# A token table made on chip by one-hot products in place of scattered writes, with gathers paced by relus

## The chip, the cores and the metric

The kernel runs on one NeuronCore of one Trainium2 chip. The metric is device time in microseconds (us). The kernel before has a median of 384.94 us in 3 runs (384.61 to 385.42). Its profile is one more execution, taken by the hardware profiler; that one took 421.93 us, of which 420.1 us lie between the first and the last instruction.

The engines are named as the profile names them: PE is TensorE's matmuls and PEld its weight loads, DVE is VectorE, ACT is ScalarE, POOL is GpSimd, and SP is SyncE, which here only issues transfers.

## What is computed

Two stages follow each other: attention with a relative position bias, and then a mixture of eight experts in which a hash of each token's id names its expert. Shapes: batch 8, 8 heads, 576 positions, head dimension 64; 4608 tokens of width 512; 8 experts with a hidden width of 1024.

```python
# attention, cut
scores = scale * np.matmul(q, k.transpose(0, 1, 3, 2))
scores = scores + bias.transpose(2, 0, 1)[None, :, :, :]
scores = scores - np.max(scores, axis=-1, keepdims=True)
attn = np.exp(scores)
attn = attn / (np.sum(attn, axis=-1, keepdims=True) + 1e-09)
attn_out = np.matmul(attn, v)
# (B, H, S, D) becomes x of (B * S, H * D); then the experts:
expert_idx = token_ids * np.int64(2654435761) % np.int64(E)
for e in range(E):
    mask = expert_idx == e
    xe = x[mask]
    h = np.maximum(xe @ w1[e], 0.0)
    out[mask] = h @ w2[e]
```

Because the multiplier is odd and E is 8, the low three bits of a token's id settle its expert.

## The kernel before

The attention stage walks through 32 pairs of heads (8 batches of 4 pairs; pair n). For each pair it goes through five groups g: TensorE makes the scores, ScalarE takes the exponential, VectorE multiplies the part near the diagonal by the exponential of the bias ("band"), and TensorE multiplies the result of the pair before by v ("av"), which VectorE divides by the row sum and writes to x_all. VectorE also converts q and k to fp16 and empties the transposes from PSUM.

A routing generator `route()` is advanced by one step after the scores of a group, in pairs 2 to 7 at most. It gives every token a slot: 640 slots for each expert (CAP), 5120 in all (NSLOT). ds2 holds the slot of each token, 128 partitions by 40 columns.

```python
def route():
    ...                       # expert of each token, its rank within the expert
    nc.vector.scalar_tensor_tensor(
        out=ds2[:, :], in0=ovf[:, :], scalar=float(BIG),
        in1=sel[:, :], op0=ALU.mult, op1=ALU.add,
    )
    yield
```

From the slots the kernel needs the opposite: for each slot, which row of x belongs there and which row of the output it goes to (the two differ, since positions are stored in a permuted order). It writes this table to memory with 40 scatters of 128 entries of 8 bytes, and reads it back as xid:

```python
def name_slot(g):
    i = nc.gpsimd.indirect_dma_start(
        out=id_d.ap()[:, :],
        out_offset=bass.IndirectOffsetOnAxis(ap=ds2[:, g : g + 1], axis=0),
        in_=pay[:, g, :], in_offset=None,
        bounds_check=NSLOT - 1, oob_is_err=False,
    )
...
for n in range(NP + 1):
    ...
    if b + 1 < B and m == 3:
        cast_vs(b + 1)              # on GpSimd
    if n >= 8:
        for g in unnamed[:3]:
            name_slot(g)
        del unnamed[:3]
    if n == 27:
        nc.sync.dma_start(out=xid[:, :, :],
                          in_=id_d.ap().rearrange("(g p) c -> p g c", p=P))
    ...
    for g in range(NIT):            # NIT is 5
        scores(n, g)
        if 2 <= n < 8:
            next(routing, None)
        if g == 0:
            transpose_k(n + 1)      # PSUM tile pk, tag "aux"
            band(n - 1, NIT - 1)
            advance(av, 13)
        elif g == 1:
            cast_v(n + 2)
            cast_k(n + 2)
            advance(av, 14)
            band(n, 0)
        elif g == 2:
            cast_q(n + 3)
            advance(av, 9)
            band(n, 1)
        elif g == 3:
            transpose_q(n + 2)      # PSUM tile pq, tag "aux"
            band(n, 2)
            advance(av, 99)
        else:
            band(n, 3)
```

The tag "aux" has two PSUM buffers, which pk, pq and the two tiles px of each pair's av take in turn:

```python
def aux(shape, dtype, name):
    return atp.tile(shape, dtype, name=name, tag="aux", bufs=2,
                    space=bass.MemoryType.PSUM)
```

In the expert stage, GpSimd gathers the rows of x for each expert (five gathers of 128 rows), TensorE transposes them, the hidden layer runs in eight groups ft that each end in a relu on ScalarE, and the second layer's results are scattered to the output:

```python
xn = {0: x_load(0)}
xt = {0: x_transpose(xn[0])}
xn[1] = x_load(1)
for e in range(E):
    if e + 2 < E:
        xn[e + 2] = x_load(e + 2)
    for ft in range(NFT):                 # 8
        ...                               # 8 matmuls into hps
        nc.scalar.activation(..., func=AF.Relu, ...)
    if e + 2 < E:
        load_w1(e + 2)
    if e + 1 < E:
        xt[e + 1] = x_transpose(xn[e + 1])
    for kc in range(NSC):                 # 5
        ...                               # 8 matmuls into ops, a copy to ok
        so = nc.gpsimd.indirect_dma_start(out=out[:, :], ...)
    if e + 2 < E:
        load_w2(e + 2)
```

Of the kernel before, what the change touches and what calls it, by code (L numbers as in the profile page):

```python
# [11 lines left out]
F32 = mybir.dt.float32  # L12
F16 = mybir.dt.float16
# [18 lines left out]
def kernel(  # L32
# [11 lines left out]
    nc = tc.nc  # L44
# [37 lines left out]
    I128_np[:PB, P:] = np.eye(PB)[:, ::-1]  # L82
    CNT_np = np.ones((P, 2 * P), dtype=np.float16)
    CNT_np[:, :P] = np.tril(CNT_np[:, :P])
    UA, UB = 2 * HALF // 3, HALF // 3
    tok_of = np.concatenate([
# [6 lines left out]
    for t in range(NIT):  # L93
# [11 lines left out]
        np.tile(np.arange(E, dtype=np.float32), (P, 1)),  # L105
    ], axis=1)

# [7 lines left out]
    x_d = nc.dram_tensor("t5_x", [N, DM], F16, kind="Internal")  # L115
    id_d = nc.dram_tensor("t5_id", [NSLOT, 2], I32, kind="Internal")

# [12 lines left out]
    flag = cst.tile([1, 1], I32, name="flag")  # L130
    cst.tile([P, 48], I32, name="gap1")

    def disjoint(x, group):
        i = getattr(x, "ins", x)
        tc.declare_no_dep(
            i, group=group,
            reason="each token has a row of its own, so these writes are disjoint",
        )
        tc.add_to_no_dep_group(group, i)
# [23 lines left out]
    with tc.tile_pool(name="at", bufs=1) as at, tc.tile_pool(  # L163
# [25 lines left out]
        tef = at.tile([P, S], F16, name="tef")  # L189
        cnt = at.tile([P, 2 * P], F16, name="cnt")  # L190
        msk = at.tile([P, NGT + E], F32, name="msk")

# [60 lines left out]
        def route():  # L253
# [14 lines left out]
            for t in range(NIT):  # L268
# [17 lines left out]
                in0=ef[:, :].unsqueeze(1).to_broadcast([P, E, NGT]),  # L286
                in1=msk[:, NGT:].unsqueeze(2).to_broadcast([P, E, NGT]),
                op=ALU.is_equal,
# [5 lines left out]
                           space=bass.MemoryType.PSUM)  # L294
            nc.tensor.matmul(out=rps[:, 0, :EN], lhsT=cnt[:, P:], rhs=ohf)
            nc.tensor.matmul(out=rps[:, 1, :EN], lhsT=cnt[:, :P], rhs=ohf)
# [43 lines left out]
                out=ds2[:, :], in0=ovf[:, :], scalar=float(BIG),  # L340
                in1=sel[:, :], op0=ALU.mult, op1=ALU.add,
            )
            yield
# [153 lines left out]

        def name_slot(g):
            i = nc.gpsimd.indirect_dma_start(  # L499
                out=id_d.ap()[:, :],  # L500
                out_offset=bass.IndirectOffsetOnAxis(
                    ap=ds2[:, g : g + 1], axis=0
                ),
                in_=pay[:, g, :],
                in_offset=None,
                bounds_check=NSLOT - 1,
                oob_is_err=False,
            )
            disjoint(i, "ids")

        def store(b, t0, t1):
# [106 lines left out]
        for i in range(1, 4):  # L618
            v_init(i)
        nobody = at.tile([P, NSLOT // P, 2], I32, name="nobody")  # L620
        nc.gpsimd.memset(nobody[:, :, :], BIG)
        load_bias(nc.gpsimd, 0, 1, 0)
        load_bias(nc.sync, 0, 1, 1)
        for b2 in range(2):
# [20 lines left out]
        )  # L645
        nc.gpsimd.dma_start(
            out=id_d.ap().rearrange("(p g) c -> p (g c)", p=P),
            in_=nobody[:, :, :].rearrange("p g c -> p (g c)"),
        )
        for i in range(3):  # L650
            nc.gpsimd.memset(xg[i][:, :, :].bitcast(I32), 0)

        NP = len(pairs)
        unnamed = list(range(NGT))
        routing = route()
# [4 lines left out]
        for n in range(NP + 1):  # L660
# [15 lines left out]
            if n >= 8 and pairs[n][1] == 0:  # L676
                store(pairs[n - 8][0], 0, NIT)
            if n >= 8:
                for g in unnamed[:3]:
                    name_slot(g)  # L680
                del unnamed[:3]
            if n == 27:
                nc.sync.dma_start(
                    out=xid[:, :, :],
                    in_=id_d.ap().rearrange("(g p) c -> p g c", p=P),
                )
            if n == 20:
# [7 lines left out]
            for g in range(NIT):  # L695
                scores(n, g)
                if 2 <= n < 8:
                    next(routing, None)
# [42 lines left out]
            if n == NP - 1:  # L741
                band(n, NIT - 1)
        assert not unnamed and next(routing, None) is None
        guard.__exit__(None, None, None)

    with tc.tile_pool(name="mo", bufs=1) as mo, tc.tile_pool(
# [5 lines left out]

        def x_load(e):
            xpn = xg[e % 3]
            for sc in range(NSC):
                nc.gpsimd.indirect_dma_start(  # L756
                    out=xpn[:, sc, :],
                    out_offset=None,
                    in_=x_d.ap()[:, :],
                    in_offset=bass.IndirectOffsetOnAxis(  # L760
                        ap=xid[:, NSC * e + sc, 0:1], axis=0
                    ),
                    bounds_check=N - 1,
                    oob_is_err=False,
                )
            return xpn
# [21 lines left out]
        xt = {0: x_transpose(xn[0])}  # L788
        xn[1] = x_load(1)
        for e in range(E):  # L790
            if e + 2 < E:
                xn[e + 2] = x_load(e + 2)
            w1h, w2h = w1t[e % 2], w2t[e % 2]
            h1 = mo.tile([P, NFT, CAP], F16, name="h1", bufs=2)
            for ft in range(NFT):
                hps = mop.tile([P, NRC, 512], F32, name="hps", bufs=2,
                               space=bass.MemoryType.PSUM)
                for nr in range(NRC):
# [9 lines left out]
                    in_=hps[:, :, :NR], func=AF.Relu, bias=0.0, scale=1.0,  # L808
                )
            if e + 2 < E:  # L810
                load_w1(e + 2)
            if e + 1 < E:
                xt[e + 1] = x_transpose(xn[e + 1])
            for kc in range(NSC):
# [20 lines left out]
                )  # L835
                disjoint(so, "orows")
            if e + 2 < E:
                load_w2(e + 2)
# [129 lines left out]
```

## Time and profile before

| What | Value |
|---|---|
| time, median of 3 | 384.94 us |
| span in the profile | 420.1 us |
| attention, up to the last store of x | about 237 us of the span |
| first matmul of the expert stage's hidden layer | 249.1 us |
| scatters of the table (40, GpSimd) | 45.7 us busy, 1.14 us each, between 51.8 and 157.3 us |
| gathers of x (40, GpSimd) | 40.8 us busy, 1.02 us each |
| scatters of results (40, GpSimd) | 39.5 us busy, 0.99 us each |

How to read it: the page gives each engine's busy time, then the span in 40 slices of 10.5 us with a digit for the busy share of each. The groups list the instructions by line, their shape, how often they ran, busy time and mean duration, and then how long the engine had been idle before them and what ended that wait. A timeline row has the start in us from the span's beginning, the duration in us, the engine and the instruction; in brackets stands the idle time before it and what it waited for. "Issue" there is time in which the engine waited for nothing that the profile shows.

### The profile page before, as it was taken

How to read it: one execution, taken by the hardware profiler on the slowest of the kernel's cores; microseconds unless marked ns; L12 is line 12 of the kernel's file. 1: busy time of each engine (PE TensorE's matmuls, PEld its weight loads, DVE VectorE, ACT ScalarE, POOL GpSimd, SP SyncE). 2: the span in 40 equal slices, each digit the busy share in tenths (PEclk: the TensorE clock that was granted, in tenths of full speed). 3: DMA queues.
4: the chain of work that ended last, by engine and by line, in shares of the span. 5: the costliest groups of instructions: out<-in, count | busy, mean ns of one | idle time of the engine just before them, and what ended most of it. 6: DMA issues, size and time to landing. Idle time of an engine off the chain costs nothing.

```text
span 420.1 us, 8668 instructions
## 1 busy us (share of the span) xinstructions
PE 340.8 (81%) x3433; PEld 241.1 (57%) x3433; DVE 232.7 (55%) x646; ACT 220.4 (52%) x258; POOL 167.5 (40%) x193
## 2 busy tenths in 40 slices
PE   2778887966865878889988456999999999999992
PEld 1457665755754767777777334564646465656550
DVE  4688885965963989999997320313141413132211
ACT  1676766965954879999999202241405050414230
POOL 5570171372372180010100175265747474640422
PEclk9898896995995999999999958999999999999997
DMA  8999646564553659899990132669798999997212
GB/s 196 235 240 250 154 104 155 141 131 119 148 113 112 155 128 183 205 238 246 198 190 3 59 95 75 107 163 206 183 209 179 218 196 205 184 203 107 111 43 84
DMA packets 124436, 65.88 MB, mean 157 GB/s; under 512 B 85215, under 2 KB 116600, under 8 KB 124386
## 3 DMA queue, kind: packets, MB, share of 16 engines
q0 software_dynamic: 19456, 31.94, 36.2%
q1 hardware_dynamic: 104834, 33.18, 33.2%
q8 instruction: 29, 0.48, 0.5%
q14 instruction: 21, 0.17, 0.2%
q10 hardware_dynamic: 96, 0.11, 0.1%
HBM read 68.26 MB, written 15.30 MB: 199 GB/s over the span
## 4 chain that ended last, share of the span: by engine, by line
PE 40%; issue 20%; ACT 14%; POOL 8%; DMA 7%; DVE 6%; SPq 2%; POOLq 1%; another core or an unknown queue 0%; ACTq 0%
ACT att L402 11%; PE hps L800 9%; PE ops L818 9%; PE px L473 8%; PE ps L394 7%; POOL out_dram L826 4%; DMA kf<-in_k_dram 4%; PE ps L398 3%; POOL xg L756 3%; ACT vt L246 3%; DMA xg<-t_x,xid 2%; PE pk L367 2%; PE xps L774 1%; DVE att L435 1%; DVE x_all L484 1%
## 5 line engine op out<-in xcount | busy, mean ns | idle before, releaser
L402 ACT ACTIVATE att<-ps 128x1152 f16<-128x1152 f32 x128 | 141.4, 1129 | 52.9 <-PE ps L398 40.8
L806 ACT ACTIVATE h<-hps 128x640 f16<-128x640 f32 x64 | 45.1, 704 | 124.9 <-PE hps L800 100.6
L394 PE MATMUL ps<-qt,kz 128*128 128x384 f16 x256 | 79.3, 348 | 28.4 <-ACT att L402 21.2
L473 PE MATMUL px<-vt,att 128*128 128x98 f16 x1280 | 86.8, 213 | 4.8 <-DVE x_all L484 2.4
L473 PEld LDWEIGHTS <-att 128*128 128x128 f16 x1280 | 74.1, 102 | 11.5 <-issue 4.0
L800 PE MATMUL hps<-xpt,w1t 128*128 128x320 f16 x512 | 75.1, 309 | 3.3 <-issue 2.3
L435 DVE TENSOR_TENSOR att<-att,ebd 128x384 f16<-128x384 f16 (+2 forms) x224 | 71.1, 354 | 3.7 <-ACT att L402 3.6
L818 PE MATMUL ops<-w2t,h 128*128 128x512 f16 x320 | 70.4, 379 | 0.0
L800 PEld LDWEIGHTS <-w1t 128*128 128x128 f16 x512 | 51.5, 101 | 26.7 <-issue 4.1
L398 PE MATMUL ps<-qt,kz 128*128 128x192 f16 x256 | 66.4, 260 | 0.0
L826 POOL DMA_INDIRECT out_dram<-ok,xid x40 | 39.5, 987 | 63.9 <-DVE ok L825 63.6
L756 POOL DMA_INDIRECT xg<-t_x,xid x40 | 40.8, 1020 | 50.3 <-DMA t_x<-x_all 38.4
L778 DVE COPY xpt<-xps 128x512 f16<-128x512 f16 x40 | 15.7, 421 | 80.5 <-PE xps L774 78.4
L825 DVE COPY ok<-ops 128x512 f32<-128x512 f32 x40 | 27.7, 691 | 52.0 <-PE ops L818 52.0
L818 PEld LDWEIGHTS <-h 128*128 128x128 f16 x320 | 31.0, 98 | 36.0
L499 POOL DMA_INDIRECT t_id<-pay,ds x40 | 45.7, 1141 | 12.1 <-issue 11.0
L224 POOL CAST vs<-vsf 64x256 f16<-64x256 f32 x16 | 8.8, 550 | 104.3 <-PE px L473 62.4
L398 PEld LDWEIGHTS <-kz 128*128 128x128 f16 x256 | 26.2, 102 | 33.8 <-issue 33.7
L473 PE MATMUL px<-vs,atts 128*128 128x132 f16 x160 | 36.3, 227 | 1.5 <-issue 1.2
L394 PEld LDWEIGHTS <-kz 128*128 128x128 f16 x256 | 26.2, 102 | 13.2 <-issue 2.9
L484 DVE TENSOR_TENSOR x_all<-px,rcp 128x256 f16<-128x256 f32 x64 | 31.4, 491 | 2.2
L774 PE MATMUL xps<-ident,xg 128*128 128x128 f16 x160 | 15.0, 229 | 15.8 <-DMA xg<-t_x,xid 12.1
(67 smaller groups left out, 289.7 us busy)
## 6 DMA issues: line engine op xcount, KB each, us to landing
qf<-in_q_dram SPq DMA_DIRECT2D x32, 288.0 KB
kf<-in_k_dram SPq DMA_DIRECT2D x32, 288.0 KB
vf<-in_v_dram SPq DMA_DIRECT2D x64, 128.0 KB
w1t<-in_moe_w_dram POOLq DMA_DIRECT2D x8, 1024.0 KB
w2t<-in_moe_w_dram POOLq DMA_DIRECT2D x8, 1024.0 KB
t_x<-x_all SPq DMA_DIRECT2D x7, 512.0 KB
vsf<-in_v_dram SPq DMA_DIRECT2D x16, 64.0 KB
t_id<-pay,ds POOLq DMA_INDIRECT x40
```

Of the source, the lines that this page charges most:

```text
L394: nc.tensor.matmul(out=ps[:, hh, :QW], lhsT=kt, rhs=qt[:, :QW], start=True, stop=True,)
L398: nc.tensor.matmul(out=ps[:, 2, RW * hh : RW * hh + RW], lhsT=kt, rhs=qt[:, QW:], start=True, stop=True,)
L402: nc.scalar.activation(out=att[:, g, :, :], in_=ps[:, :, :QW], func=AF.Exp, bias=0.0, scale=scale,)
L435: nc.vector.tensor_tensor(out=a, in0=a, in1=ebd[:, :, m, :, a0 + w0 : a1 + w0].transpose([0, 2, 1, 3]), op=ALU.mult,)
L473: nc.tensor.matmul(out=px[:, ii, o : o + w], lhsT=lhsT, rhs=rhs, start=(y == 0), stop=(y == len(todo) - 1), skip_group_check=True,)
L484: nc.vector.tensor_tensor(out=x_all[:, b, its[0] : its[0] + ni, P * m : P * m + P].rearrange("p t (h d) -> p t h d", h=2), in0=pv[:, :, :, ...
L499: i = nc.gpsimd.indirect_dma_start(out=id_d.ap()[:, :], out_offset=bass.IndirectOffsetOnAxis(ap=ds2[:, g : g + 1], axis=0), in_=pay[:, g, ...
L756: nc.gpsimd.indirect_dma_start(out=xpn[:, sc, :], out_offset=None, in_=x_d.ap()[:, :], in_offset=bass.IndirectOffsetOnAxis(ap=xid[:, NSC * ...
L800: nc.tensor.matmul(out=hps[:, nr, :NR], lhsT=w1h[:, kt, ts(ft, P)], rhs=xt[e][:, kt, ts(nr, NR)], start=(kt == 0), stop=(kt == NPT - 1),)
L806: nc.scalar.activation(out=h1[:, ft, :].rearrange("p (r n) -> p r n", r=NRC), in_=hps[:, :, :NR], func=AF.Relu, bias=0.0, scale=1.0,)
L818: nc.tensor.matmul(out=ops[:, :], lhsT=h1[:, ft, ts(kc, P)], rhs=w2h[:, ft, :], start=(ft == 0), stop=(ft == NFT - 1),)
L826: so = nc.gpsimd.indirect_dma_start(out=out[:, :], out_offset=bass.IndirectOffsetOnAxis(ap=xid[:, NSC * e + kc, 1:2], axis=0), in_=ok[:, : ...
```

## The change

The table is no longer written to memory and read back. Two one-hot factors are made on VectorE for each batch: ph says which partition a token's slot lies in, and rh which of the 40 columns. TensorE multiplies them, so that the product holds, at each slot, the token's position plus one and its batch; VectorE adds up the eight batches and turns the sums into the two columns of xid. The step of xid's second column (the output row) follows the permutation by thresholds. The steps are appended to `route()`, which now goes on at two steps for each pair (after the scores of groups 1 and 3) from pair 5.

In the expert stage, the gathers for a later expert are issued one by one, each after a tiny copy on GpSimd that reads a value of the relu's output and so waits for that relu. The gathers for expert 2 come after expert 0's results. The purpose is to take the scatters out of the attention loop and to avoid long runs of gathers.

```diff
@@ in route(), behind ds2 @@
+            part = at.tile([P, 2, NGT], I32, name="part")
+            col = at.tile([P, 2, NGT], F16, name="col")
+            nc.vector.tensor_scalar(out=part[:, 0, :], in0=ds2[:, :],
+                scalar1=P - 1, scalar2=None, op0=ALU.bitwise_and)
+            nc.vector.tensor_scalar(out=part[:, 1, :], in0=ds2[:, :],
+                scalar1=P.bit_length() - 1, scalar2=None, op0=ALU.arith_shift_right)
+            yield
+            nc.vector.tensor_scalar(out=col[:, :, :], in0=part[:, :, :],
+                scalar1=1000.0, scalar2=None, op0=ALU.min)
+            acc = at.tile([P, 2, NSG], F32, name="acc")
+            yield
+            for b in range(B):
+                ph = at.tile([P, NIT, P], F16, name="ph", tag="ohsb")
+                rh = at.tile([P, NIT, 2, NSG], F16, name="rh", tag="ebsb")
+                cb = ...                          # col of this batch
+                nc.vector.tensor_tensor(out=ph[:, :, :],          # 640 elements
+                    in0=cnt[:, 2 * P : 3 * P].unsqueeze(1).to_broadcast([P, NIT, P]),
+                    in1=cb[:, 0, :].unsqueeze(2).to_broadcast([P, NIT, P]),
+                    op=ALU.is_equal)
+                yield
+                nc.vector.tensor_tensor(out=rh[:, :, 1, :],       # 200 elements
+                    in0=cnt[:, 3 * P :].unsqueeze(1).to_broadcast([P, NIT, NSG]),
+                    in1=cb[:, 1, :].unsqueeze(2).to_broadcast([P, NIT, NSG]),
+                    op=ALU.is_equal)
+                yield
+                nc.vector.tensor_tensor(out=rh[:, :, 0, :], in0=rh[:, :, 1, :],
+                    in1=msk[:, NGT + E :].unsqueeze(2).to_broadcast([P, NIT, NSG]),
+                    op=ALU.mult)
+                nc.vector.tensor_scalar(out=rh[:, :, 1, :], in0=rh[:, :, 1, :],
+                    scalar1=float(b), scalar2=None, op0=ALU.mult)
+                yield
+                nps = aux([P, 2, NSG], F32, "nps")
+                for t in range(NIT):
+                    nc.tensor.matmul(out=nps[...], lhsT=ph[:, t, :], rhs=rh[:, t, :, :],
+                                     start=(t == 0), stop=(t == NIT - 1))
+                if b == 0:
+                    nc.vector.tensor_copy(out=acc[:, :, :], in_=nps[:, :, :])
+                else:
+                    nc.vector.tensor_tensor(out=acc[:, :, :], in0=acc[:, :, :],
+                        in1=nps[:, :, :], op=ALU.add)
+                yield
+            ...                    # ep (2 operations), xid's column 0, tk
+            for i in steps:        # three places where the permutation jumps
+                ...                # tm, and tk = tk + tm
+                yield
+            ...                    # xid's column 1 from tk
@@ in the loop over pairs @@
-            if n >= 8:
-                for g in unnamed[:3]:
-                    name_slot(g)
-                del unnamed[:3]
-            if n == 27:
-                nc.sync.dma_start(out=xid[:, :, :], in_=id_d...)
-                if 2 <= n < 8:
+                if n >= 2 and (n < 5 or g in (1, 3)):
                     next(routing, None)
@@ in the expert stage @@
-        xn[1] = x_load(1)
         for e in range(E):
-            if e + 2 < E:
-                xn[e + 2] = x_load(e + 2)
             for ft in range(NFT):
                 ...                               # matmuls and relu
+                later = e + 2 if e > 0 else 1
+                if later < E and ft < NSC:
+                    nc.gpsimd.tensor_copy(out=pace[:, :], in_=h1[:1, ft, 0:1])
+                    xn[later] = x_load(later, ft)     # one gather
             ...
+            if e == 0:
+                xn[2] = x_load(2)
```

Also removed are the table in memory, its fill and the tile for that; the constants cnt and msk grow by the numbers that the one-hots are compared and weighted with.

## The prediction

> **What bounds the kernel now.** I read the page first, then busy time by window, the groups with shapes kept apart, and the timelines of ScalarE, TensorE and VectorE.
>
> ```profile
> span 420.1 us, 8668 instructions
> PE 340.8 (81%) x3433; PEld 241.1 (57%) x3433; DVE 232.7 (55%) x646; ACT 220.4 (52%) x258; POOL 167.5 (40%) x193
> ...
> DVE  4688885965963989999997320313141413132211
> ...
> PEclk9898896995995999999999958999999999999997
> ```
>
> The averages mislead: VectorE is busy 55% of the span, but its row of slices reads 9 wherever the attention loop is undisturbed. By windows of 20 us:
>
> ```profile
> core 0: us, PE busy (x) PEld busy (x) DVE busy (x) ACT busy (x) POOL busy (x), PEclk, DMA share, GB/s
> 120.00:140.00 20.00, 11.51 (x126) 8.99 (x123) 9.66 (x30) 9.48 (x11) 7.08 (x8) 0.74 0.44 111
> 180.00:200.00 20.00, 17.26 (x257) 14.21 (x254) 19.41 (x62) 18.69 (x22) 0.00 (x0) 1.00 1.03 237
> ```
>
> The second window is the loop at its steady rate: VectorE 19.41 of 20 us. ScalarE's last exponential of each head pair gives that rate:
>
> ```profile
> 176.56 0.66 ACT L414 ACTIVATE atts<-ps 128x576 f16<-128x576 f32 x1
> 182.36 0.66 ACT L414 ACTIVATE atts<-ps 128x576 f16<-128x576 f32 x1
> 188.15 0.66 ACT L414 ACTIVATE atts<-ps 128x576 f16<-128x576 f32 x1
> ```
>
> One pair is 5.79 us. Who sets it? VectorE's timeline (start, duration):
>
> ```profile
> 184.65 0.55 DVE L240 CAST kh<-kf 96x768 f16<-96x768 f32 x1
> 185.23 0.18 DVE L483 RECIPROCAL rcp<-px 128x4 f32<-128x4 f32 x1
> 185.45 0.42 DVE L484 TENSOR_TENSOR x_all<-px,rcp 128x256 f16<-128x256 f32 x1
> 185.79 0.48 DVE L435 TENSOR_TENSOR att<-att,ebd 128x128 f16<-128x128 f16 x2
> 186.19 0.55 DVE L231 CAST qh<-qf 96x768 f16<-96x768 f32 x1
> 186.66 0.62 DVE L435 TENSOR_TENSOR att<-att,ebd 128x384 f16<-128x384 f16 x2
> ```
>
> No idle time stands on any of these lines: each instruction starts before the one ahead has reported its end, or 0.03 us after. So VectorE sets the pair, with no slack I can find. ScalarE waits some 0.5 us a pair. TensorE streams about 11,000 columns a pair (scores 5184, products with v 4580, transposes 1248); at 0.136 us per 320 columns (expert stage: 64 matmuls in 8.69 us by the chain) that is 4.6 us.
>
> The first window is different. While GpSimd issues the 40 scatters of the table (groups row: 45.7 us busy, from 51.8 to 157 us), TensorE stalls:
>
> ```profile
> 126.36 0.22 PE L473 MATMUL px<-vs,atts 128*128 128x132 f16 x1 [1.19 <-issue]
> 128.96 0.64 PE L409 MATMUL ps<-qt,kz 128*128 128x288 f16 x2 [2.38 <-issue]
> ```
>
> "Issue" means that it waited for nothing the profile shows. Such gaps stand near 61-66, 90-98, 121-131 and 152-155 us, always some 6 to 10 us into a run of back-to-back scatters, and again at 250-262 us during 15 back-to-back gathers. Removing them is what the change is for.
>
> **How much of that is in the timed run?** The profiled execution took 421.93 us; the timed ones 384.94. Line up the stalls. From pair 5's last exponential (56.73 us) to pair 31's (233.41) pass 176.7 us. Without stalls, 24 pairs at 5.79 and the two short last ones (5.39 and 5.09) make 149.4: excess 27.2. Expert 0 takes from 249.13 to 275.95, 26.8 us, against 19.8 for expert 1 (275.95 to 295.77): excess 7.0. Together 34.2, while profiled and timed differ by 37.0. The pair rate can't shrink in the timed run if VectorE bounds it, nor the expert rate at TensorE's full speed. So almost the whole of the stalls must be missing from the timed runs. The profiled stalls show 35 us to be gained, the timed kernel perhaps 0 to 5.
>
> [...]
> - [...] the 384-element fp16 product reports 0.35 us, but its neighbour starts 0.27 us later[...]. I cost by this start-to-start pitch, not by duration.
> - [...]
> - [...] PEclk 0.74 in 120-140 us, behind the stall.
> - [...]
>
> **The change part by part.**
> 1. Removed: 40 scatters on GpSimd, two small transfers around the table in memory and its fill. No engine of the steady loop waits for them except by the stalls: 0 to 5 us saved, I take 2.
> 2. Added on VectorE, per batch (eight batches).[...]
>    - is_equal ph, 640[...]: 0.67 + 0.07 = 0.74
>    - is_equal rh, 200: 0.21 + 0.07 = 0.28
>    - product with msk (fp32 operand), 200: 0.28, and about 0.1 until the in-place scaling behind it, which waits for it, may start: 0.38
>    - scaling by b, one source, 200 fp16: about 0.15
>    - accumulate from PSUM, 80: about 0.2
>
>    Sum 1.75; eight times: 14.0 us.
> 3. Added on VectorE once: part twice, col, ep twice, xid and tk, three times tm and tk, xid: 14 instructions of 40 to 80 elements at 0.11 (0.2 where one waits for the one ahead): about 2.2 us. VectorE in all: 16.2 us.
> 4. Where it lies: route is advanced five times a pair in pairs 2 to 4 (15 of 52 steps), then twice, so the other 37 end in pair 23. The order of instructions of the built kernel confirms it: ph in one pair, rh, product and scaling in the next, the matmuls and accumulate after that. All of it falls where VectorE has no slack, so it adds one to one: four steps, 1.75 us, on two pairs, 0.9 us a pair. Pairs 5 to 23 go from 5.79 to about 6.65 us.
> 5. Added on TensorE: 40 matmuls of 80 columns, under 0.1 us each: 4 us, in an engine with 1.2 us spare a pair. Their nps tile takes a turn in the two "aux" PSUM buffers, so the second px must now wait until VectorE has emptied the first. TensorE stalls perhaps 1.2 us in eight pairs, but VectorE has work then (bands, cast, and the long ph behind). I charge 0.2 us x 8 = 1.6.
> 6. Gathers: five of them follow expert 0's relus instead of coming at once; the last is issued near relu 4, some 6 us into expert 0, and lands (2.9 us from issue to the transpose in this trace) about when the transposes of expert 1 begin. From expert 1 on, GpSimd comes to its gathers only after the scatters of results, when most of those relus are done, so pacing costs a copy each. Sum 0, perhaps -0.5.
> 7. Expert stage otherwise: unchanged.
>
> Sum: 384.9 - 2 + 16.2 + 1.6 - 0.5 = 400, less about 2 us, because some small instructions fill gaps: the order places a few behind an instruction whose successor waits 0.03 to 0.1 us for its end anyway, and pair 4 still has idle time on VectorE. Predicted: 398 us.
>
> **The rivals.**
> - The stalls are real in the timed run, and the profile's extra 37 us lie elsewhere (start-up, which is full of transfers: DMA rows 8 and 9 in the first slices). Then about 34 us go and 16 come: 367. For it: the gaps start only under bursts, in both stages. Against it: start-up up to pair 5 takes 56.7 us, of which at most 10.5 exceed pairs at 5.79 behind a first one at 17.2, so no place is left for the 37.
> - VectorE's gaps are wide enough and the added work vanishes: 384 (same). Against it: 19.41 of 20 us, and starts that follow on each other. For it: part of the busy time is reported latency. I subtracted pitches, not durations, and found no gap over 0.1 us.
> - TensorE's new wait for the px buffer passes on to ScalarE (which has 0.5 us slack a pair)[...]: another 0.7 us in eight pairs[...]: 405.
>
> **Range and chances.**[...] If the stalls cost 8 us in the timed run: -6. If the wait of item 5 is exposed: +6. Hence 388 to 405. The 2% lines are 377.2 and 392.6: slower 0.80, within 0.10, faster 0.10, nearly all of the last from the first rival.
>
> **What would show it.** In the profile of the changed kernel: the "issue" gaps of TensorE in the loop gone and expert 0 near 20 us, so the profiled span shrinks, to about 403, while the timed one grows; pairs 6 to 21 at 6.4 to 6.9 us on ScalarE's last exponential; VectorE still at 9 in every slice of the loop; ph at about 0.82 us duration[...], 8 of them; a wait of px for x_all in even pairs. I am wrong if pairs stay at 5.8 us with the new instructions in place, or if the timed kernel falls with the profiled one.

## The result: 404.51 us, and a different gain on other chips

The changed kernel takes 404.51 us (median of 4 runs, 403.49 to 405.76). The kernel before took 385.18 us beside it (4 runs). The ratio is 1.0495, with a 95% interval of 1.0448 to 1.0543: slower by 5%.

The kernel before takes 385 us on some chips and about 430 us on others, and its first profile (421.93 us, with stalls) is of the second kind. The experiments ran on three chips, on one occasion each, called A, B and C here:

| Chip | before, median | runs |
|---|---|---|
| the comparison above | 385.18 | 4 |
| A | 429.75 | 15 |
| B | 385.09 | 7 |
| C | 432.29 | 6 |

A seventh run on C (437.76 us, 1.7% above the fastest there) counts as slow and is left out of the comparisons.

The page of the changed kernel's profile (the span; the engines' busy time; two rows of slices, each of 10.0 us):

```profile
span 401.7 us, 8762 instructions
...
PE 333.2 (83%) x3473; PEld 233.8 (58%) x3473; DVE 245.2 (61%) x700; ACT 220.2 (55%) x258; POOL 126.4 (31%) x181
...
DVE  4669999999999999999997112222323231313130
...
PEclk9879999999999999999999759999999999999995
```

The profiled execution is one of the timed runs here (403.49 us, of which 401.7 lie between first and last instruction). From the fourth slice on, VectorE's row is now an unbroken run of nines through the attention loop, and so is the clock's. The dips of the kernel before (8s and 5s in both rows) are gone. By windows of 20 us of the changed kernel:

```profile
core 0: us, PE busy (x) PEld busy (x) DVE busy (x) ACT busy (x) POOL busy (x), PEclk, DMA share, GB/s
120.00:140.00 20.00, 16.15 (x233) 12.62 (x232) 19.21 (x60) 16.25 (x19) 3.08 (x4) 1.00 0.81 164
180.00:200.00 20.00, 17.32 (x259) 14.43 (x258) 19.43 (x58) 18.37 (x21) 1.88 (x3) 1.00 0.80 163
```

Both windows are full of VectorE now. In the first, ScalarE has only 16.25 us of work in 20, where the loop without one-hots (second row) gives it 18.37: the pairs have become longer. ScalarE's last exponential of each pair, in the changed kernel:

```profile
109.67 0.66 ACT L525 ACTIVATE atts<-ps 128x576 f16<-128x576 f32 x1
116.33 0.66 ACT L525 ACTIVATE atts<-ps 128x576 f16<-128x576 f32 x1
122.81 0.66 ACT L525 ACTIVATE atts<-ps 128x576 f16<-128x576 f32 x1
129.46 0.66 ACT L525 ACTIVATE atts<-ps 128x576 f16<-128x576 f32 x1
```

They are 6.66, 6.48 and 6.65 us apart, against 5.79 before. VectorE's timeline inside such a pair shows where the time lies:

```profile
101.47 0.62 DVE L546 TENSOR_TENSOR att<-att,ebd 128x384 f16<-128x384 f16 x2
102.01 0.81 DVE L371 TENSOR_TENSOR ph<-cnt,col 128x640 f16<-128x640 f16 x1
102.74 0.45 DVE L471 COPY qt<-pq 128x576 f16<-128x576 f16 x1
...
106.21 0.36 DVE L380 TENSOR_TENSOR rh<-cnt,col 128x200 f16<-128x200 f16 x1
106.48 0.55 DVE L243 CAST kh<-kf 96x768 f16<-96x768 f32 x1
```

ph starts at 102.01 and its follower at 102.74: 0.73 us of the pair. rh takes 0.27 by the same reading. No idle time stands on these lines, so each one-hot pushes the rest back by its whole length.

### The profile page after: what moved, and what is told of

Its sections match the earlier page's. It is cut to its first block, busy times and chain, and to the rows that moved or that the text cites. A ratio compares the mean times of both kernels' runs of the same rounds, so it can differ in the third digit from the quotient of the medians.

```text
span 401.7 us, 8762 instructions
## 1 busy us (share of the span) xinstructions
PE 333.2 (83%) x3473; PEld 233.8 (58%) x3473; DVE 245.2 (61%) x700; ACT 220.2 (55%) x258; POOL 126.4 (31%) x181
## 4 chain that ended last, share of the span: by engine, by line
DVE 33%; PE 28%; issue 11%; DMA 9%; POOL 7%; ACT 6%; SPq 3%; POOLq 0%; ACTq 0%
PE ops L903 11%; DVE att L546 10%; PE hps L879 8%; DVE x_all L595 5%; ACT att L513 4%; POOL out_dram L911 4%; PE px L584 3%; DMA xg<-t_x,xid 3%; DMA w2t<-in_moe_w_dram 3%; DVE kh L243 3%; DVE qh L234 3%; POOL xg L838 2%; PE ps L505 2%; DVE qt L471 2%; DMA kf<-in_k_dram 2%
## 5 line engine op out<-in xcount | busy, mean ns | idle before, releaser
L584 PE MATMUL px<-vt,att 128*128 128x98 f16 x1280 | 83.1, 208 | 13.5 <-DVE x_all L595 10.9
L505 PE MATMUL ps<-qt,kz 128*128 128x384 f16 x256 | 75.1, 333 | 18.9 <-ACT att L513 17.2
L584 PEld LDWEIGHTS <-att 128*128 128x128 f16 x1280 | 69.3, 98 | 22.1 <-DVE x_all L595 13.9
L879 PE MATMUL hps<-xpt,w1t 128*128 128x320 f16 x512 | 72.8, 304 | 0.0
L509 PE MATMUL ps<-qt,kz 128*128 128x192 f16 x256 | 64.0, 250 | 0.0
L227 POOL CAST vs<-vsf 64x256 f16<-64x256 f32 x16 | 9.9, 621 | 142.4 <-PE px L584 137.5
L509 PEld LDWEIGHTS <-kz 128*128 128x128 f16 x256 | 25.3, 99 | 23.5 <-issue 23.5
L584 PE MATMUL px<-vs,atts 128*128 128x132 f16 x160 | 35.4, 222 | 0.3 <-ACT atts L525 0.3
L505 PEld LDWEIGHTS <-kz 128*128 128x128 f16 x256 | 25.3, 99 | 11.9 <-DVE kz L484 1.7
L856 PEld LDWEIGHTS <-xg 128*128 128x128 f16 x160 | 10.9, 101 | 17.5 <-DMA xg<-t_x,xid 12.1
```

The costliest lines, as they stand in the source:

```text
L505: nc.tensor.matmul(out=ps[:, hh, :QW], lhsT=kt, rhs=qt[:, :QW], start=True, stop=True,)
L509: nc.tensor.matmul(out=ps[:, 2, RW * hh : RW * hh + RW], lhsT=kt, rhs=qt[:, QW:], start=True, stop=True,)
L584: nc.tensor.matmul(out=px[:, ii, o : o + w], lhsT=lhsT, rhs=rhs, start=(y == 0), stop=(y == len(todo) - 1), skip_group_check=True,)
L879: nc.tensor.matmul(out=hps[:, nr, :NR], lhsT=w1h[:, kt, ts(ft, P)], rhs=xt[e][:, kt, ts(nr, NR)], start=(kt == 0), stop=(kt == NPT - 1),)
```

## Experiments

### Chip A: the kernel before again, without scatters, and the two halves of the change

The question was first whether the stalls belong to the profiler or to the runs, and what the one-hots and the pacing cost each by itself. The times that were expected of e2 to e4 start from a kernel before of 385 us; here it takes 430, so it is the differences that can be compared.

**e1, the kernel before, unchanged.**

> The kernel before, unchanged, with a profile of its own. Theory (the stalls of TensorE seen in the first profile, 34 us of them, are not in the timed runs): timed 385 us; the span of its profile may show either, and if it is near 383 us, all pairs from 6 on take 5.8 us in it. Rival (the stalls are always there and the timed runs are shorter elsewhere): the profile's span is again near 420 us with the same gaps at the same places, and a timed 385.

Measured: 429.37 us (12 runs), ratio to the kernel before on this chip 1.0005 (0.9977 to 1.0032). The page of that run's profile:

```profile
span 426.9 us, 8668 instructions
...
DVE  4689928964883798999998410223131414131311
...
PEclk9898977995897799999999958899999999999998
```

The span is 426.9 us, and those of the other eleven runs are 425.5 to 430.3, so the stalls are in the timed runs on this chip. Three pairs take 14.0 to 14.9 us and those behind them 7.5 to 8.2, where an undisturbed one takes 5.8. Around the first of these, in the timeline of all engines (only the scatters of the table and the starved instructions are kept):

```profile
58.70 0.98 POOL L499 DMA_INDIRECT t_id<-pay,ds  x1 [0.30 <-issue]
59.56 1.13 ACT L402 ACTIVATE att<-ps 128x1152 f16<-128x1152 f32 x1 [4.17 <-PE px L473]
59.98 0.98 POOL L499 DMA_INDIRECT t_id<-pay,ds  x1 [0.30 <-issue]
60.74 0.64 PE L409 MATMUL ps<-qt,kz 128*128 128x288 f16 x2 [2.35 <-issue]
61.27 0.98 POOL L499 DMA_INDIRECT t_id<-pay,ds  x1 [0.30 <-issue]
63.85 1.13 ACT L402 ACTIVATE att<-ps 128x1152 f16<-128x1152 f32 x1 [3.16 <-remote]
```

The scatters follow each other at 1.3 us. TensorE waits for nothing that is shown, and ScalarE waits 4.17 us for TensorE (of its second wait the profile names no cause: "remote").

**e2, no scatters at all.** This kernel leaves out the table's making: xid is loaded from a constant table with a fixed assignment of tokens, and the routing steps that give ds2 stay. Its output is not that of the reference.

```diff
-            if n >= 8:
-                for g in unnamed[:3]:
-                    name_slot(g)
-                del unnamed[:3]
             if n == 27:
-                nc.sync.dma_start(out=xid[:, :, :], in_=id_d...)
+                nc.sync.dma_start(out=xid[...], in_=XID_d.ap())   # constant
```

> The kernel before without the 40 scatters of the table, its fill and its reading back; xid comes from a fixed table of a random order with 576 tokens for each expert, so the output leaves the routing out. Nothing is added on VectorE. Theory (the scatters cost the timed kernel next to nothing): 380 to 386 us. Rival (the stalls are real in the timed run): 355 to 362 us. Either way its profile has no issue gaps of TensorE in the loop and pairs of 5.8 us.

Measured: 400.67 us, ratio 0.9336 (0.9291 to 0.9381). The pairs from 6 on take 5.8 us, but for two of 5.9 and 6.1 and the two short last ones. VectorE's row is full from the fourth slice to the end of the loop:

```profile
span 397.2 us, 8570 instructions
...
DVE  4789999999999999999861004140404040414030
```

The last exponential starts at 203.94 us, against 239.13 in e1. Expert 0, whose gathers still come in a burst, takes 29.1 us (27.6 in e1). So the scatters make the loop's stalls on this chip: some 33 us, since 2.5 of the 35.2 us lie ahead of the first scatter (50.9 us in e1). And 5.79 us is the pair where nothing is stalled, as the prediction read it.

The total fell by only 29: expert 0 was 1.4 us longer, and the last expert stage, from its first matmul to the end of the span, took 28.9 us where e1 has 25.1. No theory had foreseen that second difference.

**e3, the changed kernel without pacing.**

```diff
+        xn[1] = x_load(1)
         for e in range(E):
+            if e + 2 < E:
+                xn[e + 2] = x_load(e + 2)           # as in the kernel before
...
-                later = e + 2 if e > 0 else 1
-                if later < E and ft < NSC:
-                    nc.gpsimd.tensor_copy(out=pace[:, :], in_=h1[:1, ft, 0:1])
-                    xn[later] = x_load(later, ft)
...
-            if e == 0:
-                xn[2] = x_load(2)
```

> The changed kernel with the gathers issued in the order of the kernel before, without the copies that wait for relus. Theory (pacing is worth nothing to the timed run): 402 to 406 us, within 1% of the changed kernel. Rival (pacing saves the stall of expert 0, 7 us): 409 to 413 us. Second rival (pacing delays expert 1): 400 us or less.

Measured: 415.49 us, ratio 0.9671 (0.9626 to 0.9716). Its loop is the changed kernel's (pairs of 6.47 to 6.83), its last exponential at 219.11. From e2 to e3 only the one-hot steps come in (with the fixed table going out): +14.8 us in the time, +15.2 at the last exponential. This is the cost of the one-hots by itself. Expert 0 takes 30.0 us. The changed kernel with pacing was not run on this chip.

**e4, the kernel before with the changed kernel's pacing** (the same lines added to the kernel before).

> The kernel before with only the pacing of the gathers from the change; the scatters of the table stay. Theory: 384 to 387 us, the same as before. Rival (the stall of expert 0 is real in the timed run): 377 to 380 us. Second rival (pacing delays expert 1): 387 to 390 us.

Measured: 424.36 us, ratio 0.9886 (0.9824 to 0.9948). Expert 0 takes 22.1 us in place of 27.6, and the loop's stalls stay. So on a chip with stalls, pacing the gathers brings the 5.5 us of expert 0 and nothing in the loop; about 1.5 us is lost again in experts 1 to 6 (120.9 against 119.3).

### Chip B: the changed kernel again, and two ways to lighten it

**f1, the changed kernel, unchanged.**

> The changed kernel, unchanged, beside the kernel before in the same session. The kernel before took 385 us in the first comparison and 430 us in the second session, where its profile shows the stalls. Theory (the changed kernel holds nothing that stalls TensorE, so its time does not move with the session): 403 to 407 us, whether the kernel before is at 385 or at 430; the ratio is then 1.05 or 0.94. Rival (the whole session is slower, whatever the kernel): with the kernel before at 430 the changed one is near 450.

Measured: 402.68 us, ratio 1.0472 (1.0416 to 1.0528). The kernel before takes 385.09 here, the same as in the first comparison. Its 7 runs have spans of 382.0 to 385.1 us, which leaves no room for stalls: e2's last exponential without any (203.94) and what f2, below, needs from there to the end (179.3) make 383.2. The kernel before was not profiled here, so this is an inference from its spans. The changed kernel's pairs are the same as ever. On this chip, experts 1 to 6 take 19.35 us each.

**f2, the 40 scatters spread instead of replaced.** The kernel before, with two scatters a pair from pair 8, each behind a small copy on GpSimd that reads a finished part of x_all and so waits for it; gathers paced as in e4; xid read at pair 28.

```diff
-            if n >= 8:
-                for g in unnamed[:3]:
-                    name_slot(g)
-                del unnamed[:3]
-            if n == 27:
+            if n == 28:
                 ...                                        # xid is read back
+                if n >= 8 and g in (2, 4) and unnamed:     # in the loop over g
+                    nc.gpsimd.tensor_copy(out=pace[:, :], in_=x_all[:1, ...])
+                    name_slot(unnamed.pop(0))
```

> The kernel before with its 40 scatters kept, but issued two a pair from pair 8, each after a one-element copy on GpSimd that reads what VectorE last wrote to x_all; gathers paced as in the change; nothing added on VectorE. Theory (a run of back-to-back indirect transfers stalls TensorE, not their number): no issue gaps of TensorE in the loop, pairs of 5.8 us, 384 to 398 us. Rival (each scatter costs TensorE its share, however spaced): about as long as the kernel before with paced gathers, 424 us where the kernel before takes 430.

Measured: 387.82 us, ratio 1.0107 (1.0023 to 1.0191). Pairs take 5.8 to 5.9 us (pair 28, where xid is read back, 6.5), so spread scatters cost the loop next to nothing: the last exponential is at 206.56. Whether spreading removes stalls could not be seen here, since the kernel before shows no room for any on this chip; g1, on chip C, can show it.

**f3, the changed kernel with the conversions of q and k moved to GpSimd** from pair 6 on, to free VectorE.

```diff
-            nc.vector.tensor_copy(out=qh[n]...)
+            (nc.gpsimd if n >= 6 else nc.vector).tensor_copy(out=qh[n]...)
-            nc.vector.tensor_copy(out=kh[n]...)
+            (nc.gpsimd if n >= 6 else nc.vector).tensor_copy(out=kh[n]...)
```

> The changed kernel with the two fp16 conversions of q and k on GpSimd from pair 6 on, which takes 0.47 and 0.58 us a pair off VectorE by its starts. Theory (VectorE sets the pair): pairs with one-hot steps fall from 6.66 to 5.5 to 5.8 us, those without to 5.2 to 5.5 us, and the time to 380 to 390 us. Rival (the 6.66 us come from the wait of px for the shared PSUM buffer or from elsewhere): pairs stay above 6.4 us, 400 us or more. Second rival (GpSimd slows VectorE when both work): in between.

Measured: 401.48 us, ratio 1.0449 (1.0389 to 1.0509), 0.3% below f1, whose runs it overlaps (401.13 to 404.29 against 401.87 to 404.72). Pairs with one-hot steps fell from 6.66 to 6.47 on average, not by the 1 us that the two conversions take. These are the numbers that the first rival named, but not by its cause: VectorE is still full where one-hots are made (first row), and has some slack only behind them (second row):

```profile
100.00:120.00 20.00, 16.91 (x250) 13.63 (x247) 19.40 (x55) 16.76 (x19) 6.17 (x8) 1.00 0.62 159
180.00:200.00 20.00, 17.80 (x264) 14.74 (x262) 17.72 (x53) 18.01 (x22) 5.50 (x7) 1.00 0.85 166
```

Groups of f3 with shapes kept apart (count, then busy time and mean ns):

```profile
L546 DVE TENSOR_TENSOR att<-att,ebd 128x640 f16<-128x640 f16 x64 | 39.9, 623 | 2.9 <-ACT att L513 2.9
...
L595 DVE TENSOR_TENSOR x_all<-px,rcp 128x256 f16<-128x256 f32 x32 | 13.6, 425 | 1.1
...
L396 DVE TENSOR_SCALAR rh<-rh 128x200 f16<-128x200 f16 x8 | 6.3, 784 | 0.3
```

The same from f2, where VectorE makes the conversions:

```profile
L436 DVE TENSOR_TENSOR att<-att,ebd 128x640 f16<-128x640 f16 x64 | 31.1, 486 | 1.8 <-ACT att L403 1.8
...
L485 DVE TENSOR_TENSOR x_all<-px,rcp 128x256 f16<-128x256 f32 x32 | 13.6, 424 | 1.1
```

The band products of 640 elements, which read two fp16 tensors in SBUF, grew from 486 to 623 ns in the mean, and the in-place scaling from the changed kernel's 222 to 784. The division, which reads one operand from PSUM, stayed at 425. Inside f3's trace, the 36 of these 64 products that overlap a conversion on GpSimd take 732 ns in the mean, the other 28 take 483; the division of 384 elements takes 558 either way. ph takes 819 ns in the mean, against 814 in the changed kernel, but only one of the eight overlaps a conversion, so it doesn't tell whether ph would be hit. Why the products are longer there was not shown. The freed time is mostly given back: counted by starts in pairs 12 to 19, the conversions free 0.99 us a pair, the 640-element products take 0.39 of it back and the one-hot steps 0.42, which leaves about the 0.19 that were seen.

**f4, f2 with the conversion of k alone on GpSimd.**

```diff
-            nc.vector.tensor_copy(out=kh[n]...)
+            (nc.gpsimd if n >= 6 else nc.vector).tensor_copy(out=kh[n]...)
```

> As the one with paced scatters, and the conversion of k on GpSimd from pair 6 on, which takes 0.58 us a pair off VectorE. Theory: 0.3 to 0.5 us a pair less than with paced scatters alone, until ScalarE (5.3 us a pair) bounds the loop: 10 us less in all. Rival (GpSimd, with scatters and conversions, becomes late, or slows VectorE): no gain, or slower.

Measured: 408.76 us, ratio 1.0606 (1.0558 to 1.0654). GpSimd now has scatters, their copies and conversions in one queue. The conversion comes late, TensorE waits 8.7 us for kh, and single pairs take up to 13.3 us. This way beats neither kernel.

### Chip C: is it the spacing? And what lengthens the end?

**g1, f2 once more**, where the stalls are.

> The kernel before with its 40 scatters spread at two a pair, each behind a small copy on GpSimd, and the gathers behind relus, once more, because the session decides what it can show. If the kernel before takes about 385 here, it stalls nowhere and this kernel again takes 386 to 390. If it takes 425 to 430, the stalls are there. Theory A (back-to-back runs of indirect transfers make them): the spaced scatters don't, pairs of 5.8 to 6.0, last exponential near 206, time 386 to 394, ratio near 0.91. Theory B (each scatter costs the same wherever it stands): the loop keeps most of its excess of some 25 to 35 us, time 412 to 425, last exponential above 225.

Measured: 398.94 us, ratio 0.9215 (0.9125 to 0.9306). The kernel before takes 432.29 here. The page of g1:

```profile
span 397.4 us, 8808 instructions
...
DVE  4679999997897999988986103132323222222221
...
PEclk9989999998998999999999579999999999999998
```

The last exponential is at 214.50 us. Six pairs of the loop take 6.7 to 8.0, the others 5.8: about 8 us more than f2 has on chip B, where e1 has some 33 more than e2 on chip A. Neither theory holds whole: the time lies 5 us above what theory A (back-to-back runs) named and 13 below theory B (a cost of each scatter, wherever it stands); the last exponential, 8.5 above A's 206 and 10.5 below B's 225, is nearly in the middle. So with the same 40 scatters, spacing takes away roughly three quarters of the loop's stalls (a comparison across chips, as no profile of the kernel before was taken on C). A quarter stays though the scatters are spread; why some pairs are hit and most are not is open. g1 is the fastest kernel of this chip; on chip B it is 1% behind the kernel before.

**g2, the changed kernel, unchanged.**

> The changed kernel beside it. It takes 401 to 406 in every session so far. So the ratio to the kernel before is 1.04 to 1.05 where that takes 385, and 0.94 where it takes 430: theory A says that nothing in the changed kernel depends on the session, since it has neither bursts in the loop nor long runs of gathers. The last drain on GpSimd takes 4.32 us.

Measured: 410.78 us, ratio 0.9479 (0.9390 to 0.9567). The ratio came as foreseen, the time did not: 410.78 lies above 401 to 406. The loop is the same (last exponential at 219.35). The expert stage is longer: expert 1 takes 23.2 us and experts 1 to 6 together 123.0, against 116.1 in f1: the changed kernel, too, depends on the chip, which theory A had ruled out. TensorE's timeline of g2 in expert 1:

```profile
265.96 0.61 PE L856 MATMUL xps<-ident,xg 128*128 128x128 f16 x8
268.31 0.38 PE L856 MATMUL xps<-ident,xg 128*128 128x128 f16 x4 [1.73 <-DVE xpt L860]
...
270.04 10.48 PE L903 MATMUL ops<-w2t,h 128*128 128x512 f16 x40
```

and GpSimd's in the same stretch:

```profile
258.31 0.98 POOL L911 DMA_INDIRECT out_dram<-ok,xid  x1 [0.75 <-DVE ok L910]
259.60 1.06 POOL L838 DMA_INDIRECT xg<-t_x,xid  x1 [0.30 <-issue]
...
266.82 0.18 POOL L891 CAST pace<-h 1x1 f32<-1x1 f16 x1
267.17 1.04 POOL L838 DMA_INDIRECT xg<-t_x,xid  x1 [0.18 <-issue]
268.20 0.18 POOL L891 CAST pace<-h 1x1 f32<-1x1 f16 x1
268.54 1.02 POOL L838 DMA_INDIRECT xg<-t_x,xid  x1 [0.16 <-issue]
```

The pacing copies wait for nothing here (0.18 us, no wait for the relu): GpSimd reaches them when those relus are long done. The results' scatters, the gathers for expert 2 and those for expert 3 thus follow each other closely, the gathers from 259.6 to 273.6 us at 1.3 to 1.4 us each, with one transfer of weights between. Some 7 us into these TensorE starts to stall (shown as a wait for VectorE's copy), and 40 matmuls take 10.48 us where they take 8.80 in expert 0. That this run of transfers makes the stall is argued from the times alone. It doesn't settle the size: g4, below, has the same run at the same place on the same chip, and its expert 1 takes 20.2 us; f1 has it on chip B and takes 19.35. The prediction had noted that pacing costs only a copy each from expert 1 on; what it means on a chip with stalls it had not.

A smaller part of the difference between chips shows in every kernel: experts 2 to 5 mostly take 20.0 to 20.5 us on A and C and 19.35 on B. Expert 6, in which no gather is left, takes 19.35 on all three.

**g3, the changed kernel with 40 scatters that nothing reads**, spaced as in f2. They write a table in memory of their own.

```diff
+                if n >= 8 and g in (2, 4) and unnamed:
+                    nc.gpsimd.tensor_copy(out=pace[:, :], in_=x_all[:1, ...])
+                    name_slot(unnamed.pop(0))
```

> The changed kernel with 40 scatters added that nothing reads, two a pair from pair 8, each behind a small copy on GpSimd. Theory N (the drain at the end depends on the number of indirect transfers, 120 in the kernel before, 80 in the changed one): the drain goes back to 1.54 us and the stretch from the last expert's first matmul to the end to 25.7 us from 28.8, so if the loop stays as it is, the time falls from about 403 to about 400. Theory X (the drain belongs to something else that the change did): 4.32 us stays, and the time stays or rises by 1 to 3 us for the scatters.

**g4, the same with 8**, one a pair in pairs 24 to 31 (`n >= 24 and g == 2`).

> The changed kernel with 8 scatters added that nothing reads, one a pair in pairs 24 to 31. Theory N with a length that falls evenly with the number: the drain is 4.32 - 8 x 0.069 = 3.76 us and the time 402 to 403. With a step somewhere between 80 and 120: 4.32 or 1.54. Theory P (it is enough that there are scatters to a second table): 1.54 us and about 400. Theory X: 4.32 us, and the time of the changed kernel.

Measured: g3 413.40 us, ratio 0.9539 (0.9462 to 0.9616); g4 408.95 us, ratio 0.9444 (0.9355 to 0.9533). GpSimd's program ends with an instruction DRAIN, behind the last scatter. Its length, and the time from the last expert's first matmul to the end, from the traces:

```
kernels                          indirect transfers   drain        last expert to the end
before, e1, e4, f2, f4, g1              120            1.54 us         25.1 to 26.0 us
g3 (changed kernel + 40)                120            1.54            25.3
changed kernel, e2, e3, f1, f3, g2       80            4.32            28.5 to 29.1
g4 (changed kernel + 8)                  88            4.48            29.2
```

g3 brings the short drain back in the changed kernel, so theory X falls. g4 rules out that the presence of such scatters is enough (theory P), and a fall in proportion: 8 more transfers made it 0.16 us longer. The drain's length goes with the number of indirect transfers at the three numbers tried: 4.32 us at 80, 4.48 at 88, 1.54 at 120. The instruction ahead of it (INC_SWDGE_SEM) goes the same way: 1.24, 1.28 and 0.56 us. Where they turn, and why, is open. g3's gain at the end was outweighed: its loop from pair 5 takes 170.7 us against 164.0 in g2, in five pairs of 7.0 to 8.3 us as in g1. The 8 scatters of g4 cost its loop nothing (164.0).

## Why the prediction held, step by step

The time, 404.5 against 398 predicted, is inside the range, half a microsecond below its upper end, and the direction is right. The cost of the one-hots was worked out and measured. That the sign held took luck as well: the comparison fell on runs in which the kernel before takes 385 us. The prediction would be wrong "if the timed kernel falls with the profiled one", and on chip C it does. By its steps:

- **VectorE sets the pair, with no slack.** Right. e2, without scatters, runs at 5.8 us a pair, with VectorE at nine in every slice of the steady loop; adding VectorE work lengthened the pairs.
- **Items 2 to 5, the one-hots: 16.2 + 1.6 - 2 of gaps filled = 15.8 us.** Measured by e3 against e2: 14.8 in the time, 15.2 at the last exponential. Groups of the changed kernel with shapes kept apart:

```profile
L371 DVE TENSOR_TENSOR ph<-cnt,col 128x640 f16<-128x640 f16 x8 | 6.5, 814 | 0.0
L380 DVE TENSOR_TENSOR rh<-cnt,col 128x200 f16<-128x200 f16 x8 | 2.9, 358 | 0.0
L389 DVE TENSOR_TENSOR rh<-rh,msk 128x200 f16<-128x200 f16 x8 | 2.8, 356 | 0.0
L396 DVE TENSOR_SCALAR rh<-rh 128x200 f16<-128x200 f16 x8 | 1.8, 222 | 0.3
L412 DVE TENSOR_TENSOR acc<-acc,nps 128x80 f32<-128x80 f32 x7 | 1.7, 238 | 1.1 <-PE nps L403 1.1
```

  ph's start-to-start pitch is 0.735 us (0.74 predicted), rh's 0.277 (0.28), the product's 0.390 (0.38), the scaling's 0.138 (0.15). The accumulation has a pitch of 0.155 (about 0.2), and ahead of it VectorE waits 0.16 us for TensorE's product, 1.1 us in seven instructions, which the prediction had not counted. The rate put for ph, 0.67 us for its 640 elements, was an estimate. The kernel before shows two rates:

```profile
40.92 0.48 DVE L320 TENSOR_TENSOR rnk<-rnk,oh 128x320 f16<-128x320 f32 x1
41.32 0.55 DVE L231 CAST qh<-qf 96x768 f16<-96x768 f32 x1
...
44.68 0.48 DVE L435 TENSOR_TENSOR att<-att,ebd 128x640 f16<-128x640 f16 x1
45.08 0.19 DVE L334 SCALAR_TENSOR_TENSOR sel<-ef,rank 128x40 f32<-128x40 f32 x1
```

  A product of 320 elements that is partly fp32 and an fp16 band product of 640 elements both take 0.40 us from start to start. The band products of 128, 384 and 640 elements take 0.13, 0.27 and 0.40, which is 0.07 us and 0.52 ns for each element; with the same 0.07, the first product takes 1.04 ns for each. ph, all fp16, goes at the slower of the two: 0.735 us for 640 elements is 0.07 and 1.04 ns for each. At the other rate its eight would have taken 2.7 us less. What makes ph slower than the band products was not shown.
- **Item 4, pairs of 6.65 us from 5 to 23.** Right: pairs 5 to 23 average 6.61. From 7 to 20 they go 6.47, 6.66, 6.82, 6.66 in turn, as the steps fall; 21 to 23 take 6.1 to 6.3.
- **Item 5, the second px waits for VectorE.** The wait is there, about as large as thought. The group of the changed kernel:

```profile
L584 PE MATMUL px<-vt,att 128*128 128x98 f16 x1280 | 83.1, 208 | 13.5 <-DVE x_all L595 10.9
```

  It is 10.9 us in 19 waits, of at most 0.9 (the kernel before has 2.4 us of it), where I had put 1.2 us in each of eight pairs, 9.6 in all. How much of it reaches the end was not separated; the sum of items 2 to 5 leaves little room for more than the 1.6 charged.
- **Item 1, 2 us saved from stalls.** Nothing shows this gain where the kernel before takes 385. f2, whose scatters stall nothing, is no faster than it.
- **Item 7, "Expert stage otherwise: unchanged".** This is the term that was mis-sized most: 0 was put, 3 came. The end of the kernel grew by 3 us in every kernel with 80 indirect transfers (28.9 in f1 against 25.7 in f2), because GpSimd's DRAIN takes 4.32 us instead of 1.54. g3 undid it by the number of transfers alone. With 3 us for the end and 0 in place of -2, the sum is 403, and the 1.5 us that are left are within the spread of the runs (403.49 to 405.76).
- **Item 6.** Expert 0 takes 21.5 us ("near 20" had been said), against 19.35 for each of the next six.
- **The stalls "must be missing from the timed runs".** Right for those runs, and the number stands. But that the stalls come with the profiler finds no support: on chip A the profiled run is as long as the others (span 426.9 us in e1, the others 425.5 to 430.3), and on chip B the spans of all runs leave no room for stalls. The profile of before and the runs beside it were of different kinds of occasion.
- **The clock, "PEclk 0.74 in 120-140 us, behind the stall".** In the profile of before the granted clock is 0.50 from 127.3 to 137.5 us. TensorE's longest idle stretch in the loop ends at 128.96 us, inside that time, and is 2.4 us; gaps of 1.7 and 1.2 us lie ahead of it and one of 2.3 behind. So the low clock comes with several gaps close together. What sets it was not shown.
- **The first rival (367 us: stalls real, 34 gone, 16 added)** describes the other kind of chip in its sign: there the changed kernel is faster by 21.5 us on chip C (432.29 to 410.78), and unpaced by 14.3 on chip A. It would be 18 by the rival's sum.

What stays open: why the stalls appear on two chips and not on a third (one occasion each, so chip and occasion aren't told apart), what in TensorE is held up, and why the part that is left in g1 stays.

## What to carry to other kernels

Where one engine sets the rate with no slack, work moved onto it costs its start-to-start pitch in full: added elements and instruction counts gave 15.8 us ahead of time, and 14.8 came. Before a change is aimed at stalls, look whether the timed runs have them: compare the profile's span with the runs' times, and repeat the kernel before on other occasions, since here the same change is 5% slower or 5% faster by that alone. If bursts of indirect transfers stall other engines, spread them first: the same 40 scatters at two a pair took about three quarters of the loop's stalls away (judged across two chips) and cost 1% where there were none, while their replacement on the busiest engine cost 5%; and a pacing copy spaces nothing if what it waits for is already done (in g2's expert 1 it takes 0.18 us, and the gathers follow each other at 1.3 to 1.4).

## What the runs showed of the hardware that was not expected

- The same kernel takes 385, 430 and 432 us on three chips, with mean granted clocks of 0.966 to 0.979, 0.926 to 0.940 and 0.918 to 0.925. On chip A most of the difference is stalls of TensorE during back-to-back indirect transfers issued by GpSimd: with 40 of them taken out of the loop (e2), 29 us go, and with the gathers of expert 0 paced (e4), 5.4. On chip C the kernel before was not profiled.
- In e1 and in the profile of before, TensorE's gaps of more than 1 us in the loop begin 7.5 us or more after a run of scatters has begun; most show as waiting for nothing (7 of 11 in the profile of before, of at most 2.4 us), with ScalarE waiting for TensorE beside it (4.17 us in e1).
- GpSimd's DRAIN at the end takes 1.54 us after 120 indirect transfers and 4.32 after 80, the same to 0.01 us in every kernel with that number and on every chip, and 4.48 after 88 (one kernel).
- In f3, VectorE's products of two fp16 tensors in SBUF (640 elements) take 732 ns in the mean when they overlap a conversion on GpSimd and 483 when they don't; a division with an operand in PSUM takes 558 either way.
